# The last weight pieces of a decode kernel: full rows of 128 on all DMA engines in place of a piece for three engines alone

## The chip, the cores and the metric

One core of one Trainium2 chip. The time is the device time of a whole execution in microseconds (us), median of several runs; the span of the profile is some 1.3 us shorter.

## The reference, cut to what matters

A decode step for 4 tokens: gated mix of a windowed attention over a key and value cache and a gated feed-forward. What matters here is how much must be loaded and what comes last.

```python
q = (x @ wq)                                   # 32 heads of 128
o = softmax(q k^T * 128**-0.5) v               # last 4096 positions, 4 batches x 8 kv heads
a = o.reshape(4, 4096) @ wo                    # wo is 4096 x 512, bf16: 4 MB
b = ((relu(x @ W_gate)) * (x @ W_up)) @ W_down
out = g * a + (1 - g) * b
```

Some 81 MB are read: keys and values, five weight matrices. `wo` is used last and is loaded last.

## The kernel before

The load order ends with `W_down` and then `wo`, all issued from SyncE. `wo` lies in SBUF as 128 rows (partitions) of 32 KB, in 64 columns of 512 B, and comes in pieces of columns, so that the matmuls of one piece run while the next piece lands:

```python
WO_PIECES = ((0, 34), (34, 52), (52, 60), (60, 63), (63, 64))
LOW3 = (0, 123, 126, 128)
...
def wo_rows(p):
    return [slice(a, b) for a, b in zip(LOW3, LOW3[1:])] if p == len(WO_PIECES) - 1 else [slice(0, 128)]
...
for n, r in enumerate(wo_rows(it[1])):
    load(("WO", it[1], n), f"d_wo{it[1]}", Wo[r, OW * lo:OW * hi], wo[r, OW * lo:OW * hi], waits=w)
```

The last column is cut into 123, 3 and 2 rows, which puts it on the three lowest DMA engines alone; the other thirteen have 4 KB less to do. TensorE adds all columns into one accumulator, even columns into its first half and odd ones into its second. The two halves are placed on different parts of the array, so that two neighbouring columns run side by side (in the trace of before the second of a pair starts 3 to 4 ns after the first):

```python
def WO(p):
    lo, hi = WO_PIECES[p]
    w = [("WO", p, n) for n in range(len(wo_rows(p)))] + [("E", "OQ")]
    for x in range(lo, hi):
        i, j = x // OUTT, x % OUTT
        mm(banks[ACC][OR * j:OR * j + 4, 0:OW], oq[:, i, :], Wo[:, OW * x:OW * x + OW], False, i == 31,
           ev=("WOP", p) if x == hi - 1 else None, waits=w if x == lo else (), pos=(0, OR * j))
```

ScalarE copies the first half and VectorE the second, and then the output is stored. TensorE's order before the wo pieces is: last attention value product (PV), down projection of the feed-forward (FFN), fold of the heads (OQ). After OQ, VectorE scales the heads into `oq`, which all wo matmuls need.

Of the kernel before, what the change touches and what calls it, by code (L numbers as in the profile page):

```python
# [24 lines left out]
OUTT = 2  # L25
OW = 512 // OUTT
OR = 128 // OUTT
WO_PIECES = ((0, 34), (34, 52), (52, 60), (60, 63), (63, 64))
LOW3 = (0, 123, 126, 128)

class _Plan:

# [17 lines left out]
def bc(ap, axis, n):  # L50
    shape = list(ap.shape)
    shape[axis] = n
    return ap.broadcast_to(shape)
# [31 lines left out]
def bass_gated_mix__sliding_block_cached__glu_gated_reglu__decode_kernel(  # L85
    nc, A_x, A_k_cache, A_v_cache, A_wq, A_wo, B_x, B_W_gate, B_W_up, B_W_down, gate_w, out
):
    plan = _Plan()
    aps = (A_x, A_k_cache, A_v_cache, A_wq, A_wo, B_W_gate, B_W_up, B_W_down, gate_w, out)
    with ExitStack() as ctx:  # L90
        R = _alloc(nc, ctx)
        progs = _program(nc, plan, R, aps)
        for _, prog in progs:
            prog(None)
        for name in plan.unit:
            plan.sems[name] = ctx.enter_context(nc.semaphore(name))
        plan.emit, plan.n = True, {}
        if True:
            for name, prog in progs:
                prog(getattr(nc, name))  # L100
# [46 lines left out]
def _order():  # L147
# [7 lines left out]
    o += [("SC", s, 3), ("SW", s), ("PV", s - 1), ("PT", s), ("RS", 1), ("GU",), ("PV", s), ("FFN",), ("OQ",)]  # L155
    return o + [("WO", p) for p in range(len(WO_PIECES))]


def _dma_order():
    o = [("wq",), ("x",), ("gw",), ("k", 0), ("k", 1), ("v", 0)]  # L160
    for s in range(2, NSET):
        o += [("k", s), ("v", s - 1)]
    return o + [("wg",), ("wu",), ("v", NSET - 1), ("wd",)] + [("wo", p) for p in range(len(WO_PIECES))]

# [22 lines left out]
def _program(nc, plan, R, aps):  # L187
# [14 lines left out]
    def slot(*it):  # L202
        return slots[:, at[it], :]
# [4 lines left out]
    Wo = slot("wo", 0)  # L208
# [19 lines left out]
    def tr(key):  # L228
        return TR[trf[key] % NTR]
# [5 lines left out]
    def scb(key):  # L235
        return SCB[scf[key] % NSC]
# [2 lines left out]
        n = scf[key] - NSC  # L239
        return [("E",) + sck[n]] if n >= 0 else [("INIT",)]  # L240

    def wo_rows(p):

        return [slice(a, b) for a, b in zip(LOW3, LOW3[1:])] if p == len(WO_PIECES) - 1 else [slice(0, 128)]

    def set_of(s):
        return s % 4, s // 4

    def ob(s):
        return banks[OB[s % 2]]  # L250

    def sync(e):
        E = _Eng(plan, e, "sp")

        def load(ev, ctr, dst, src, waits=()):
            E.op(lambda: e.dma_start(dst, src), ev=ev, waits=waits, ctr=ctr)  # L256

        for it in _dma_order():
            k = it[0]
            w = slot_wait.get(it, [])  # L260
            if k == "x":
                load(("X",), "d_x", xsb[0:4, :], A_x.rearrange("b o d -> (b o) d"))
            elif k == "gw":
                load(("GW",), "d_gw", xsb[4:5, :], gate_w.rearrange("(o p) -> o p", o=1))
            elif k == "wq":
                load(("WQ",), "d_wq", slot("wq"), A_wq.rearrange("(p t) f -> p (t f)", t=4), waits=w)
            elif k == "wg":
                load(("WG",), "d_wg", Wg, B_W_gate.rearrange("(p t) f -> p (t f)", t=4), waits=w)
            elif k == "wu":
                load(("WU",), "d_wu", Wu, B_W_up.rearrange("(p t) f -> p (t f)", t=4), waits=w)  # L270
            elif k == "wd":
                load(("WD",), "d_wd", Wd, B_W_down.rearrange("(p i) c -> p (i c)", i=14),
                     waits=w)
            elif k == "wo":
                lo, hi = WO_PIECES[it[1]]
                wo = A_wo.rearrange("(p i) c -> p (i c)", i=32)
                for n, r in enumerate(wo_rows(it[1])):
                    load(("WO", it[1], n), f"d_wo{it[1]}", Wo[r, OW * lo:OW * hi], wo[r, OW * lo:OW * hi], waits=w)
            else:
                b, qq = set_of(it[1])  # L280
                src = (A_k_cache if k == "k" else A_v_cache)[b, 4 * qq:4 * qq + 4, SK - WIN:SK, :]
                load((k.upper(), it[1]), f"d_{k}{it[1] % 3}", slot(*it), src.rearrange("h (r c) d -> r h (c d)", r=32),
                     waits=w)
        load(("OUT",), "d_out", out.rearrange("b o d -> (b o) d"), osum[:, :], waits=[("OSUM", 1), ("OSUM", 0)])
        E.wait([("OUT",)])
# [30 lines left out]
    def tensor(t):  # L316
        E = _Eng(plan, t, "pe")

        def mm(out_, lhsT, rhs, start, stop, ev=None, waits=(), pos=None):
            E.op(lambda: t.matmul(out_, lhsT, rhs, start=start, stop=stop, tile_position=pos, skip_group_check=True),  # L320
                 ev=ev, waits=waits)
# [101 lines left out]

        def WO(p):
            lo, hi = WO_PIECES[p]
            w = [("WO", p, n) for n in range(len(wo_rows(p)))] + [("E", "OQ")]
            for x in range(lo, hi):
                i, j = x // OUTT, x % OUTT
                mm(banks[ACC][OR * j:OR * j + 4, 0:OW], oq[:, i, :], Wo[:, OW * x:OW * x + OW], False, i == 31,
                   ev=("WOP", p) if x == hi - 1 else None, waits=w if x == lo else (), pos=(0, OR * j))  # L430

        fns = dict(CONST=CONST, XT=XT, Z=Z, Q=Q, QT=QT, SC=SC, PV=PV, SW=SW, RS=RS, OQ=OQ, WO=WO, GU=GU, FFN=FFN)
        for it in order:
            if it[0] in fns:
# [41 lines left out]
    def q_dst(n, u):  # L476
        return (pe, sc)[n][:, :].rearrange("p (x u w) -> p x u w", x=8, u=4)[:, :, u, :]

    def q_src(n):
        return banks[scb(("Q", n))].rearrange("p (x w) -> p x w", x=8)  # L480

    def vector(v):
# [93 lines left out]
        def FIN():  # L576
            E.op(lambda: v.tensor_copy(osum[:, OW:2 * OW], banks[ACC][OR:OR + 4, 0:OW]), ev=("OSUM", 1),  # L577
                 waits=[("WOP", len(WO_PIECES) - 1)])

# [5 lines left out]
    def scalar(a):  # L585
        E = _Eng(plan, a, "act")

        def EQ(n):
            key = ("Q", n)
            E.op(lambda: a.activation(q_dst(n, slice(0, 4)), bc(q_src(n).unsqueeze(2), 2, 4), ACTF.Copy), ev=("QD", n),  # L590
                 waits=[key])
            plan.ev[("E", "Q", n)] = plan.ev[("QD", n)]

        def ECONST(k):
            key = ("CONST", k)
            dst = consts[k]
            E.op(lambda: a.activation(dst[:, :], banks[tr(key)][:, 0:dst.shape[1]], ACTF.Copy), ev=("E",) + key, waits=[key])

        def GWB():
            E.op(lambda: a.activation(R["gwB"][:, :, :], bc(xT[:, 4:20:5].unsqueeze(2), 2, 128), ACTF.Copy), ev=("GWB",),  # L600
                 waits=[("E", "XT")])

        def NORM(s):
            E.op(lambda: a.activation(osb[:, s, :], ob(s), ACTF.Copy), ev=("NORM", s),  # L604
                 waits=[("PV", s)])

        def GE():
            for u in range(2):
                E.op(lambda u=u: a.activation(ge[:, u, :], banks[ACC][:, 0:4], ACTF.Exp, scale=-1.0 if u == 0 else 1.0),
                     ev=("GE",) if u else None, waits=[("Z",)])  # L610

        def RELU():
            E.op(lambda: a.activation(grelu, banks[scb(("GU", 0))][:, 0:448], ACTF.Relu), ev=("RELU",),
                 waits=[("GU", 0), ("EXP", NSET - 1)])
            plan.ev[("E", "GU", 0)] = plan.ev[("RELU",)]

        def EXP(s):
            w = [("NEGMAX", s), ("E", "SC", s, 3)] + ([("E", "PT", s - 1)] if s else [("QT", 1, 1)])
            E.op(lambda: a.activation(pe[:, :], sc[:, :], ACTF.Exp, bias=negmax[:, s % 2:s % 2 + 1], scale=SCALE,  # L619
                                      accum_out=rowsum[:, s:s + 1]), ev=("EXP", s), waits=w)  # L620

        def FIN():
            E.op(lambda: a.activation(osum[:, 0:OW], banks[ACC][0:4, 0:OW], ACTF.Copy), ev=("OSUM", 0),
                 waits=[("WOP", len(WO_PIECES) - 2)])

        fns = dict(ECONST=ECONST, GWB=GWB, EQ=EQ, GE=GE, RELU=RELU, EXP=EXP, NORM=NORM, FIN=FIN)
        for it in act:
            fns[it[0]](*it[1:])

    return [("tensor", tensor), ("vector", vector), ("scalar", scalar), ("gpsimd", gpsimd), ("sync", sync)]  # L630


# [26 lines left out]
```

## Time and profile before

| | before |
|---|---|
| time | 196.12 us (196.02 to 196.21) |
| span of the profile | 194.8 us |
| read from memory | 81.01 MB at 416 GB/s over the span |
| the one load queue | 97.3% of its 16 engines' span |
| TensorE, VectorE, ScalarE busy | 62%, 64%, 14% |

Some words used from here on: a load is split over DMA engines; each sends a 4 B semaphore packet after its own data, and that shows as one *count* on the load's semaphore. The last count is the *landing*. A *late* engine is one whose counts come some 0.8 us or more behind those of the others.

These are lines of the timeline of before: start us, duration us, engine, line of the program (here the helper that issues every matmul), operation and operands, count, and in brackets how long the engine sat idle and what ended it.

```profile
178.49 5.03 PE L320 MATMUL bank<-slots,pT 128*64 128x512 bf16 x32 [5.70 <-DMA slots<-in_A_v_cache_dram]
183.45 1.69 PE L320 MATMUL bank<-slots,hg 128*4 128x256 bf16 x28
185.07 1.93 PE L320 MATMUL bank<-osb,fold 128*64 128x256 bf16 x16
...
188.07 2.02 PE L320 MATMUL bank<-slots,oq 128*4 128x256 bf16 x34 [1.06 <-DMA slots<-in_A_wo_dram]
190.83 1.15 PE L320 MATMUL bank<-slots,oq 128*4 128x256 bf16 x18 [0.73 <-DMA slots<-in_A_wo_dram]
192.20 0.82 PE L320 MATMUL bank<-slots,oq 128*4 128x256 bf16 x12 [0.23 <-DMA slots<-in_A_wo_dram]
```

PV, FFN, OQ, then the wo pieces.

### The profile page before, as it was taken

Reading aid. Unit: us, or ns where it says so; the run is one execution under the profiler, and the core shown is the slowest. Engines: PE = TensorE matmul, PEld = TensorE weight load, DVE = VectorE, ACT = ScalarE, POOL = GpSimd, SP = SyncE. Lnnn points to the kernel's source line nnn. Section 1 sums busy time; section 2 is a strip of 40 time slices with the busy share of each in tenths; the row PEclk is TensorE's granted clock in tenths of the full one; section 3 lists DMA queues with packets and bytes.
Section 4 is the critical chain, followed back from the end, with each engine's and each line's share of the span. In section 5 each row is a group of like instructions: output and inputs, shape, how many; then the busy total and the mean of one; then the engine's idle time right before and its main releaser. Section 6 shows DMA issues by size and latency. Waiting matters only on the chain.

```text
span 194.8 us, 1734 instructions
## 1 busy us (share of the span) xinstructions
PE 120.6 (62%) x723; PEld 50.6 (26%) x723; DVE 124.1 (64%) x153; ACT 27.5 (14%) x34; POOL 9.5 (5%) x25
## 2 busy tenths in 40 slices
PE   0209279474943894686468943894586466743974
PEld 0003123121411341242112411341142122311562
DVE  6103769999399809980998199819981998370010
ACT  2213000040130013001300130013001300420100
POOL 7830000000000000000000000000000000000000
PEclk9999958999999797899876999697999889997899
DMA  6999999999999999999999999999999999999992
GB/s 215 431 432 431 437 437 431 431 427 451 431 437 437 446 427 424 431 437 431 431 431 431 427 424 437 444 437 431 431 431 421 431 395 427 470 431 384 425 404 90
DMA packets 3616, 81.10 MB, mean 416 GB/s; under 512 B 401, under 2 KB 666, under 8 KB 794
## 3 DMA queue, kind: packets, MB, share of 16 engines
q1 hardware_dynamic: 3610, 81.01, 97.3%
q8 instruction: 5, 0.08, 0.2%
q14 instruction: 1, 0.01, 0.0%
HBM read 81.01 MB, written 0.00 MB: 416 GB/s over the span
## 4 chain that ended last, share of the span: by engine, by line
DMA 54%; DVE 31%; PE 9%; issue 4%; SPq 0%; ACT 0%
DMA slots<-in_A_k_cache_dram 38%; DVE kt L491 21%; DMA slots<-in_A_wo_dram 10%; PE bank L320 7%; DMA xsb<-in_A_x_dram 6%; DVE sc L527 5%; DVE qblk L517 1%; PE bank L324 1%; DVE pT L542 1%; DVE rd L531 1%; SPq L256 0%; DVE negmax L537 0%; ACT gwB L600 0%; DVE osum L577 0%; DVE mx L527 0%
## 5 line engine op out<-in xcount | busy, mean ns | idle before, releaser
L491 DVE STREAM_TRANSPOSE kt<-slots 128x2048 f32<-128x2048 f32 x32 | 73.7, 2305 | 28.1 <-DMA slots<-in_A_k_cache_dram 28.0
L320 PE MATMUL bank<-kt,qblk 128*128 128x512 bf16 x256 | 72.1, 434 | 27.9 <-DVE kt L491 27.9
L320 PEld LDWEIGHTS bank<-kt,qblk 128*128 128x128 bf16 x256 | 25.2, 107 | 69.7 <-DVE kt L491 36.0
L320 PE MATMUL bank<-slots,pT 128*64 128x512 bf16 x256 | 32.3, 410 | 5.7 <-DMA slots<-in_A_v_cache_dram 5.7
L619 ACT ACTIVATE pe<-sc,negmax 128x2048 bf16<-128x2048 bf16 x8 | 16.0, 2002 | 60.1 <-DVE negmax L537 60.1
L527 DVE CUSTOM_DVE_ANT_0 sc<-bank,maskf 128x512 bf16<-128x512 f32 x32 | 21.0, 658 | 3.8 <-PE bank L320 3.7
L320 PEld LDWEIGHTS bank<-slots,pT 128*64 128x64 bf16 x256 | 15.1, 118 | 23.2 <-issue 13.4
L542 DVE STREAM_TRANSPOSE pT<-pe 128x2048 bf16<-128x2048 bf16 x8 | 18.5, 2312 | 2.2 <-ACT pe L619 2.2
L604 ACT ACTIVATE osb<-bank 128x512 bf16<-128x512 f32 x8 | 4.8, 597 | 81.5 <-PE bank L320 81.5
L320 PE MATMUL bank<-rd,grpb 128*128 128x32 bf16 x8 | 1.6, 194 | 22.1 <-DVE rd L531 22.1
L555 DVE TENSOR_TENSOR oq<-bank,recip 64x128 bf16<-64x128 f32 x2 | 0.9, 434 | 12.3 <-PE bank L320 12.2
L320 PEld LDWEIGHTS bank<-rd,grpb 128*128 128x128 bf16 x8 | 0.8, 98 | 25.7 <-DVE rd L531 25.7
L495 DVE COPY xT<-bank 128x20 bf16<-128x20 bf16 x1 | 0.2, 171 | 8.0 <-PE bank L324 8.0
L320 PE MATMUL bank<-slots,oq 128*4 128x256 bf16 x64 | 4.0, 272 | 2.0 <-DMA slots<-in_A_wo_dram 2.0
L320 PE MATMUL bank<-slots,xT 128*4 128x512 bf16 (+1 forms) x64 | 5.0, 467 | 0.0
L320 PE MATMUL bank<-maskr,maskl 128*128 128x512 bf16 x1 | 0.6, 609 | 5.9 <-POOL maskr L296 5.9
L517 DVE TENSOR_SCALAR qblk<-bank 32x64 uint32<-32x64 uint32 x16 | 2.9, 215 | 2.1 <-PE bank L324 2.1
L324 PE MATMUL bank<-identb,xsb 5*128 5x5 bf16 x4 | 0.3, 168 | 5.7 <-DMA xsb<-in_A_x_dram 5.7
L577 DVE CAST osum<-bank 4x256 bf16<-4x256 f32 x1 | 0.4, 418 | 5.2 <-PE bank L320 5.2
L320 PEld LDWEIGHTS bank<-slots,oq 128*4 128x4 bf16 x64 | 2.5, 84 | 3.5 <-DMA slots<-in_A_wo_dram 2.9
L296 POOL TENSOR_SCALAR_AFFINE_SELECT fold<-fold 128x256 bf16<-128x256 bf16 x8 | 3.3, 417 | 1.1
L486 DVE MEMSET qblk<- 128x2304 uint32 x1 | 2.0, 1978 | 1.3 <-PEq L644 1.3
(59 smaller groups left out, 40.3 us busy)
## 6 DMA issues: line engine op xcount, KB each, us to landing
slots<-in_A_k_cache_dram SPq DMA_DIRECT2D x8, 4096.0 KB, 25.1
slots<-in_A_v_cache_dram SPq DMA_DIRECT2D x8, 4096.0 KB, 30.5
slots<-in_A_wq_dram SPq DMA_DIRECT2D x1, 4096.0 KB, 12.4
slots<-in_A_wo_dram SPq DMA_DIRECT2D x1, 2176.0 KB, 17.1
slots<-in_B_W_gate_dram SPq DMA_DIRECT2D x1, 1792.0 KB, 19.7
slots<-in_B_W_up_dram SPq DMA_DIRECT2D x1, 1792.0 KB, 23.6
slots<-in_B_W_down_dram SPq DMA_DIRECT2D x1, 1792.0 KB, 18.5
slots<-in_A_wo_dram SPq DMA_DIRECT2D x1, 1152.0 KB, 19.5
```

The source lines that it names most:

```text
L296: op(lambda: e.affine_select(dst, src, pattern, cmp, fill, base=base, channel_multiplier=mult), ev)
L320: E.op(lambda: t.matmul(out_, lhsT, rhs, start=start, stop=stop, tile_position=pos, skip_group_check=True), ev=ev, waits=waits)
L324: E.op(lambda: t.transpose(out_, in_, idn), ev=ev, waits=waits)
L486: E.op(lambda: v.memset(qblk[:, :, :, :, :].rearrange("p s h c e -> p (s h c e)"), 0.0), ev=("QZ",))
L491: E.op(lambda: v.transpose(kt[:, f, :].bitcast(FP32), slot("k", s)[:, 4096 * f:4096 * f + 4096].bitcast(FP32)), ev=("E", "KT", s, f), waits=w)
L517: E.op(lambda dst=dst, r=r, g=g: v.tensor_scalar(dst, src[r, g, 0:B, :, :], 0, None, op0=ALU.bitwise_or), ev=("E",) + keys[1] if (q, g) == ...
L527: E.op(lambda: v.tensor_tensor_reduce(sc[:, 512 * f:512 * f + 512], banks[scb(key)], R["maskf"][:, :], 1.0, -3.0e38, ALU.add, ALU.max, mx4 ...
L531: E.op(lambda: v.tensor_tensor(rd32[:, :, :], bc(R["own8"][:, :].unsqueeze(2), 2, 4), bc(mx4[:, :].unsqueeze(1), 1, 8), ALU.mult), ev=("MA ...
L542: E.op(lambda: v.transpose(pT[:, s % 2, :], pe[:, :]), ev=("E", "PT", s), waits=[("EXP", s)] + ([("PV", s - 2)] if s >= 2 else []))
L555: E.op(lambda g=g, r=r: v.tensor_tensor(oq[r, :, :].rearrange("p i b -> p b i"), banks[tr(key)][0:64, 128 * g:128 * g + 128].rearrange("p ...
L604: E.op(lambda: a.activation(osb[:, s, :], ob(s), ACTF.Copy), ev=("NORM", s), waits=[("PV", s)])
L619: E.op(lambda: a.activation(pe[:, :], sc[:, :], ACTF.Exp, bias=negmax[:, s % 2:s % 2 + 1], scale=SCALE, accum_out=rowsum[:, s:s + 1]), ev= ...
```

## The change

The intent is to drop the special piece: five pieces in full rows of 128, so that all 16 engines end together, with a last piece of 1 KB rows.

```diff
-WO_PIECES = ((0, 34), (34, 52), (52, 60), (60, 63), (63, 64))
-LOW3 = (0, 123, 126, 128)
+WO_PIECES = ((0, 35), (35, 52), (52, 59), (59, 62), (62, 64))
@@
-                for n, r in enumerate(wo_rows(it[1])):
-                    load(("WO", it[1], n), f"d_wo{it[1]}", Wo[r, OW * lo:OW * hi], wo[r, OW * lo:OW * hi], waits=w)
+                load(("WO", it[1]), f"d_wo{it[1]}", Wo[:, OW * lo:OW * hi], wo[:, OW * lo:OW * hi], waits=w)
@@
-            w = [("WO", p, n) for n in range(len(wo_rows(p)))] + [("E", "OQ")]
+            w = [("WO", p), ("E", "OQ")]
@@ (ScalarE's closing copy)
-                 waits=[("WOP", len(WO_PIECES) - 2)])
+                 waits=[("WOP", len(WO_PIECES) - 1)])
```

More of the change, by code (lines that the diff above doesn't have):

```diff
@@ L240, in sc_free @@
         return [("E",) + sck[n]] if n >= 0 else [("INIT",)]
-    def wo_rows(p):
-        return [slice(a, b) for a, b in zip(LOW3, LOW3[1:])] if p == len(WO_PIECES) - 1 else [slice(0, 128)]
     def set_of(s):
```

## The prediction

> **What bounds the kernel now.** I read the page's busy rows first, then the chain of work that ended last, then the stretches of the last microseconds, then the DMA issues, and last the trace's own records of single packets and of completion counts.
>
> ```profile
> DMA  6999999999999999999999999999999999999992
> q1 hardware_dynamic: 3610, 81.01, 97.3%
> DMA 54%; DVE 31%; PE 9%; issue 4%; SPq 0%; ACT 0%
> ```
>
> The DMA row is at 9 in 38 of 40 slices, and the one queue fills 97.3% of its 16 engines' span. The 81 MB set the time; DVE and PE in the chain are work that lets the next load start, not a bound of their own. The change moves no byte away, so only how the bytes end, engine by engine, can matter. The end of the chain of work says what ends last:
>
> ```profile
> 171.74 20.41 DMA slots<-in_A_wo_dram
> 192.16 0.04 issue
> 192.20 0.87 PE bank L320 x12
> 193.07 0.02 issue
> 193.09 0.42 DVE osum L577
> ```
>
> From the third-last wo piece (landed 192.16) on, only twelve matmuls, one copy and the store are left. The stretches of those microseconds (columns: us, busy of PE, PEld, DVE, ACT, POOL, granted clock, DMA share, GB/s) show the engines dropping out one after another, not together:
>
> ```profile
> 189.00:190.00 1.00, 1.00 (x21) 0.67 (x16) 0.00 (x0) 0.00 (x0) 0.00 (x0) 1.00 0.99 399
> 190.00:191.00 1.00, 0.27 (x6) 0.15 (x6) 0.00 (x0) 0.00 (x0) 0.00 (x0) 1.00 0.73 273
> 191.00:192.00 1.00, 0.97 (x18) 0.56 (x14) 0.00 (x0) 0.00 (x0) 0.00 (x0) 1.00 0.39 132
> ```
>
> So the end belongs to a few late engines. The completion counts in the trace give the rest. The 1.5 KB-row piece (the fourth) is counted by ten engines from 190.70 to 191.23, by one at 191.88, and by five from 192.35 to **192.60**. The eight counts of the last, 512 B-row piece come from 191.87 to **192.39**. Thus the last landing is the fourth piece's on the late engines, not the last piece's on the low three: the low three have some 0.2 us to spare.
>
> Why five or six are late is also in the trace. Beside 81 MB of data there are five 16 KB instruction packets (1.02 to 1.07 us each, at 40.2, 73.0, 111.7, 148.2 and 182.1 us) and one of 8 KB at 63.3. After each, one more of the 16 counts of the next big load is late: by some 1.4 us after a 16 KB packet in the middle of the run, and by 0.9 us after the 8 KB one. They stay late to the end.
>
> **What the Trainium skill says.**
> 1. "DMA: Bandwidth & Descriptors", section "Why a DMA increments its semaphore by 16 and not by 1": a DMA issued here runs on the largest number of engines up to 16 that divides its outer dimension, the lowest-numbered ones; 128 rows give 16. So 123 rows should run on 3, 3 rows on 3, and 2 rows on 2. The trace agrees: 8 landings for the last piece, plus three jumps at its issues. The 512 B packets run as three interleaved streams starting at 190.30, 190.31 and 190.32.
> 2. Same page, section "Why small descriptors are slow (HBM only)": a fixed cost per packet. The trace agrees, and its sizes are used below: the step from packet to packet on one engine is 23.5 ns at 512 B, 61.2 at 1536 B, 155.4 at 4096 B, about 646 at 17408 B. A line through these is 4.6 ns + 0.0369 ns per byte, so an estimate for 1 KB is 42.3 ns.
> 3. Same page, section "Anatomy of one DMA — SWDGE (gpsimd) path": most of a DMA's fixed cost of about 2 us is the receipt of the last write. This kernel's loads are not of that path; the trace has 0.48 us from the late engine's last semaphore packet (ends 192.118) to its count (192.596). I use 0.48.
>
> **The change part by part.** Wo has 64 column pieces of 512 B in each row; every engine serves 8 rows.
>
> *Removed:* the 123, 3 and 2 row transfers of 512 B rows: 43 or so packets of 23.5 ns on each of the three low engines, about 1.0 us there. They lie beside the late engines' work and end 0.2 us before them, so on the path they are worth 0. Also two issues by SyncE; its last two groups are issued at 173.05 (10.32 us long) and 183.42 (1.31), so all is issued by 184.8, while the first 512 B packet starts at 190.30. Worth 0.
>
> *Added:* 512 B more per row on all the other 13 engines, in 5 pieces of full rows instead of 4. Per row, on a late engine:
> - before 17408 + 9216 + 4096 + 1536 B: 4 x 4.6 + 0.0369 x 32256 = 1208.6 ns
> - after 17920 + 8704 + 3584 + 1536 + 1024 B: 5 x 4.6 + 0.0369 x 32768 = 1232.1 ns
>
> The difference is 23.5 ns; 8 rows make 188 ns, and one more 4 B semaphore packet (about 9 ns) makes **0.197 us**. The last landing goes from 192.60 to about 192.79.
>
> *Moved:* what PE does after it. Before, the fourth piece's three matmuls and the last piece's one start 0.041 us after 192.596, in two pairs (192.637 and 192.747), and the last is over at 193.023: 0.427 us from landing to end. After, the last piece has two matmuls, which start as one pair (one writes each half of the accumulator): 0.041 + 0.004 + 0.272 = 0.317 us. So 0.110 us come back. Is PE free by then? The third piece now ends at 236 KB of 256 KB per engine instead of 240, the fourth at 248 instead of 252: both about 0.15 us sooner, 192.01 and 192.45. Seven matmuls in four pairs of 0.109 us from 192.05 are through at 192.49, three more at about 192.71, before 192.83. PE is free, and the landing alone counts.
>
> *The closing copies:* ACT now waits for the last piece, as DVE always did. ACT's copy began at 193.056 and DVE's at 193.090, with 0.373 and 0.418 us (the two osum rows); DVE ends last now and will after. Worth 0. The store after it is the same.
>
> Sum: +0.197 - 0.110 = **+0.087 us**. On a median of 196.12 that is 196.2, 0.04% slower, which is inside the spread of the three runs of before (196.02 to 196.21).
>
> The instruction listing of the two kernels shows the same number of rows on PE, DVE, ACT and POOL and two fewer on SP; PE's 723 matmuls stay. Nothing before the wo loads changes.
>
> **The rivals.**
> - *The low three engines did set the end, and freeing them is a gain.* Then the time would fall by up to the 0.2 us by which I have them early, to about 195.9. Against: the 12 matmuls run with the last one paired to its neighbour (it starts 4 ns after it), so it waited for nothing of its own. A weaker form of it: three streams of 512 B reads disturb the late engines. Between 191.06 and 191.42 packets of all sizes take longer (4096 B up to 199 ns instead of 159), some 0.1 us in all on a late engine. If the small packets cause this, the change gives 0.1 back and ends at 196.1. Against: the three streams run 0.7 us before that without any such effect.
> - *The small packets cost more than the line says.* 13 engines now end in eight 1 KB packets. The only 1 KB packets of the trace, in the store, are 46 to 52 ns long. At 52 instead of 42, eight rows add 0.08 us: 196.3.
> - *The instruction packets fall elsewhere.* If one engine got two of them, it would be another 1.3 us late, and the time 197.5. If they held no engine up at the end, the last landing could come some 1.4 us sooner, with the ten early ones: 194.8. For this: nothing says how an engine is chosen. Against: PE's instruction stream, which needs most of the fetching, keeps its count, and six packets met six different engines. I give it one chance in twenty.
>
> **How the range and the chances follow.** The worked sum gives 196.21; the weaker rival pulls it to 196.1 and the second pushes it to 196.3; runs of one kernel lie within 0.1 of their median. Another day's run of the same kernel may differ by another 0.2 or so (a guess). So 195.9 to 196.5 in 8 of 10 cases. Being 2% off would take 3.9 us; no term above is larger than the 1.4 of an instruction packet. So within 2%: 0.98; faster and slower 0.01 each.
>
> **What would show it right or wrong.** In the issues of the profile after: the 192 KB piece lands near 192.45, and a 128 KB piece near 192.79 (both within 0.1 us), with 16 counts, five or six late ones among them. In the stretch from 191 to 192 the DMA share rises a little. In the chain, PE's last group has two or five matmuls, and the copy by DVE starts near 193.18. I am wrong in mechanism if the last landing comes at or before 192.60, if PE waits longer than 0.05 us after it, or if ACT's copy ends after DVE's; and wrong in size if a 1 KB step is not near 42 ns, or if the late engines are not the same number.

## The result, and the profile after

| | before | after |
|---|---|---|
| time, median | 196.12 us (196.02 to 196.21, 6 runs) | 196.11 us (195.94 to 196.19, 6 runs) |
| ratio of the fast runs | | 0.9998, 95% interval 0.9985 to 1.0011 |
| span of the profile | 194.8 us | 194.7 us |

A ratio is the mean time of one kernel's fast runs over that of the other's in the same rounds, so it is not quite the ratio of the medians; all ratios in this document are against the kernel before. The change made no difference that the timing could resolve (0.13%, or 0.25 us).

The load queue of after looks as it did, in the page's busy row and its queue row:

```profile
DMA  6999999999999999999999999999999999999992
q1 hardware_dynamic: 3618, 81.01, 97.3%
```

The end of the chain of work does not (start us, duration us, what):

```profile
188.63 0.45 DVE oq L549
189.08 0.14 issue
189.21 3.69 PE bank L314 x64
192.90 0.02 issue
192.92 0.42 DVE osum L571
```

Where before had a DMA of 20.41 us and then twelve matmuls, this trace has all 64 wo matmuls in one run of 3.69 us behind VectorE's scaling; no load is in the last part of the chain. The timeline of after shows why: its first lines answer to those of before.

```profile
178.51 6.15 PE L314 MATMUL bank<-slots,pT 128*64 128x512 bf16 x32 [5.73 <-DMA slots<-in_A_v_cache_dram]
184.59 1.69 PE L314 MATMUL bank<-slots,hg 128*4 128x256 bf16 x28
186.21 1.94 PE L314 MATMUL bank<-osb,fold 128*64 128x256 bf16 x16
...
189.21 3.67 PE L314 MATMUL bank<-slots,oq 128*4 128x256 bf16 x64 [1.06 <-DVE oq L549]
```

PV started at the same time but took 6.15 us instead of 5.03, so everything behind it came 1.1 us later, and the wo pieces were there when TensorE came. In the stretches (us, busy of PE, PEld, DVE, ACT, POOL with counts, granted clock, DMA share, GB/s) the clock of before and then of after is

```profile
178.40:183.00 4.60, 4.51 (x30) 2.45 (x32) 0.00 (x0) 0.00 (x0) 0.00 (x0) 0.68 1.01 425
```

```profile
178.40:183.00 4.60, 4.49 (x22) 2.32 (x24) 0.00 (x0) 0.00 (x0) 0.00 (x0) 0.50 1.01 425
```

0.68 against 0.50 of full clock in the same stretch. It is not the change that made that: in the repeats below the kernel before has 0.50 too, and the kernel after 0.66.

The loads end one after another as before, in the stretches of after:

```profile
189.00:190.00 1.00, 0.79 (x16) 0.68 (x18) 0.07 (x1) 0.00 (x0) 0.00 (x0) 1.00 0.97 386
190.00:191.00 1.00, 1.00 (x24) 0.83 (x20) 0.00 (x0) 0.00 (x0) 0.00 (x0) 1.00 0.73 273
191.00:192.00 1.00, 1.00 (x24) 0.83 (x20) 0.00 (x0) 0.00 (x0) 0.00 (x0) 1.00 0.35 128
```

The DMA share falls as before (there 0.99, 0.73 and 0.39), while TensorE has no gap. The completion counts show 10 early and 6 late engines again. The last landing is at 192.563 us, 0.033 **earlier** than in before (192.596) where 192.79 was foretold. So two things had to be found out: what took the 0.2 us away, and how often TensorE, not the loads, sets the end.

### The profile page after: what moved, and what is told of

It reads as the page before. It is cut to its first block, busy times and chain, and to the rows that moved or that the text cites. A ratio compares the mean times of both kernels' runs of the same rounds, so it can differ in the third digit from the quotient of the medians.

```text
span 194.7 us, 1732 instructions
## 1 busy us (share of the span) xinstructions
PE 122.7 (63%) x723; PEld 51.9 (27%) x723; DVE 124.6 (64%) x153; ACT 27.5 (14%) x34; POOL 9.5 (5%) x25
## 4 chain that ended last, share of the span: by engine, by line
DMA 46%; DVE 25%; PE 21%; issue 6%; SPq 0%; ACT 0%
DMA slots<-in_A_k_cache_dram 25%; PE bank L314 19%; DVE kt L485 18%; DMA slots<-in_A_v_cache_dram 15%; DMA xsb<-in_gate_w_dram 6%; DVE sc L521 4%; PE bank L318 2%; DVE qblk L511 1%; DVE oq L549 0%; DVE rd L525 0%; DVE negmax L531 0%; SPq L251 0%; ACT gwB L594 0%; DVE osum L571 0%; DVE mx L521 0%
## 5 line engine op out<-in xcount | busy, mean ns | idle before, releaser
L314 PE MATMUL bank<-slots,pT 128*64 128x512 bf16 x256 | 34.0, 426 | 5.7 <-DMA slots<-in_A_v_cache_dram 5.7
L314 PEld LDWEIGHTS bank<-slots,pT 128*64 128x64 bf16 x256 | 15.7, 123 | 24.9 <-issue 15.8
```

The costliest lines, as they stand in the source:

```text
L314: E.op(lambda: t.matmul(out_, lhsT, rhs, start=start, stop=stop, tile_position=pos, skip_group_check=True), ev=ev, waits=waits)
```

## The experiments

All outputs were correct. Besides the times, each run gives one trace, from which these are read: the last landing, the start of the wo matmuls, and single packets.

### Both kernels once more: chance or change?

No edit: `rep_before`, `rep_after` (3 rounds each), and later one single look each, `rep2_before` and `rep2_after`.

> The kernel before once more, unchanged, for a second trace. Theory A (the worked +0.197 us on a given late engine is right, and in the two traces it was cancelled by chance: which engine the last instruction packet hit, and a 0.1 us slowing at 191.06 to 191.42): the last landing of the 1.5 KB-row piece differs from 192.60 by more than 0.05 us, and packets of 180 ns and more near 191 us need not come back. Rival B (the change itself takes the 0.2 us away, for example because the 512 B streams on three engines slow the others): the last landing is 192.60 again within 0.05, with slow packets near 191.2 again. Time 196.1 under both.

> The kernel after once more, unchanged. Theory A: a late engine takes 5.35 us from the w_down landing to the first wo piece, as in the first trace of after (5.20 in that of before), but the last landing may lie anywhere from 192.5 to 192.9. Rival B: last landing 192.56 within 0.05. Where the granted clock in the stretch 178.4 to 183.0 is 0.5 again, PE runs 64 wo matmuls without a gap (3.7 us); where it is 0.7 or more, PE waits for the pieces. Time 196.1 under both.

> The kernel before, a third trace: slow packets near 191.3 again if the transfers on three engines make them; the last landing anywhere from 192.5 to 192.9 if chance moves it by 0.2 us.

> The kernel after, a third trace: no 3584 B packet over 160 ns after 190.0; the last landing anywhere from 192.5 to 192.9; PE without a gap in the wo stage where the clock of the stretch 178.4 to 183.0 is near 0.5.

Measured: 196.09 us (ratio 1.0001) and 196.13 us (0.9998, 0.9984 to 1.0013). The traces, with those of two later variants that have TensorE early (`before_ffn`; `ffn_split` and `ffn_split2`, further down):

| trace | clock 178.4 to 183.0 | wo matmuls start | waits among them | last landing | from it to the last matmul's end | first piece to last landing | longest 1536 B packet after 190.0 |
|---|---|---|---|---|---|---|---|
| before | 0.68 | 188.07 | yes | 192.596 | 0.427 us | 4.590 us | 95 ns |
| rep_before | 0.50 | 189.80 | none | 192.807 | 0.649 | 4.597 | 94 |
| rep2_before | 0.65 | 188.19 | yes | 192.704 | 0.428 | 4.618 | 87 |
| before_ffn | 0.69 | 188.05 | yes | 192.604 | 0.428 | 4.602 | 78 |
| after | 0.50 | 189.21 | none | 192.563 | 0.319 | 4.546 | 69 |
| rep_after | 0.66 | 188.29 | yes | 192.768 | 0.318 | 4.538 | 69 |
| rep2_after | 0.50 | 189.53 | none | 192.814 | 0.374 | 4.552 | 67 |
| ffn_split | 0.53 | 188.22 | yes | 192.721 | 0.321 | 4.545 | 67 |
| ffn_split2 | 0.50 | 188.54 | yes | 192.642 | 0.319 | 4.540 | 67 |

"First piece to last landing" runs from the last count of the first wo piece to the last landing of all. The rest is in microseconds from the span's start.

Three readings. First, the last landing moves by 0.2 us among traces of one kernel (192.60 to 192.81 and 192.56 to 192.81), so the early landing of the first trace of after was within chance. Rival B, that the landing is fixed for each kernel, is out.

Secondly, a part is not chance: first piece to last landing is 4.59 to 4.62 us in all of the old scheme and 4.54 to 4.55 in all of the new, though a late engine moves the same 14848 B per row in it under both (9216 + 4096 + 1536, and 8704 + 3584 + 1536 + 1024). With one packet per row and one semaphore packet more, the new scheme should take 0.046 us longer there, and it takes some 0.06 less. The slow packets come back in every trace of the old scheme and in none of the new.

They are not the whole of it. The packets can be linked to engines by their times. On the engine that lands last, the time from the end of the first piece's semaphore packet to the end of the last one is 4.575 us on average under both schemes (4.56 to 4.60 and 4.57 to 4.58). There the slow packets cost 0.03 to 0.07 us in the old scheme, and at most 0.02 in the new, which about pays for the extra packet per row. The other 0.06 us lie between semaphore packets and counts: on average 0.44 us after the first piece and 0.47 after the last in the old scheme, 0.46 and 0.43 in the new. No run shows what sets that delay.

Thirdly, where the clock was 0.5 in the two kernels as they are, TensorE ran its 64 wo matmuls without a wait, and where it was 0.65 or more it waited. In rep_before this cost time:

```profile
189.66 0.14 issue
189.80 3.70 PE bank L320 x64
193.50 0.02 issue
193.52 0.42 DVE osum L577
```

Its landing was over at 192.81, but its last matmul ended 0.65 us later, and this was the slowest of its four executions (196.51 us; the others 196.03 to 196.14). In rep_after the loads set the end, as the prediction had it:

```profile
171.46 19.43 DMA slots<-in_A_wo_dram
190.89 0.04 issue
190.94 2.17 PE bank L314 x29
193.10 0.02 issue
193.13 0.42 DVE osum L571
```

### full512: the sizes of before, all in full rows

```diff
-WO_PIECES = ((0, 35), (35, 52), (52, 59), (59, 62), (62, 64))
+WO_PIECES = ((0, 34), (34, 52), (52, 60), (60, 63), (63, 64))
```

(against after)

> After with the piece sizes of before: 17, 9, 4, 1.5 and 0.5 KB rows, all five on 128 rows; so it is before with the last piece spread over all 16 engines. Theory B' (transfers on few engines slow the packets of the others near 191 us; small packets as such don't): no packet of 4096 B over 172 ns and none of 1536 B over 72 ns after 190.0. Rival: the 512 B packets themselves do it, then slow ones come back in as many numbers as in the two traces of before. Last landing 0.18 after the 1.5 KB piece, anywhere from 192.6 to 192.9. Time 196.1 (within 0.15) under both.

Measured: 196.16 us, ratio 1.0001 (0.9987 to 1.0014). In its trace the clock was 0.50 again, and TensorE, not the loads, set the end (64 wo matmuls in one run from 189.43, the last over 0.66 us after the landing), so the packets are what this run is read for. After 190.0 us no 4096 B packet is over 169 ns and no 1536 B packet over 68 ns, with 128 packets of 512 B on all engines. So 512 B packets do not slow the others; transfers that run on three engines do. The last landing was earlier than foretold (192.42), as chance and the lighter first piece have it. Its first piece to last landing is 4.692 us; the packet terms give 8 x (344.2 + 155.5 + 61.2 + 23.5) ns = 4.675 us, plus four semaphore packets of 9 ns: 4.71. For after they give 8 x (325.3 + 136.7 + 61.2 + 42.3) = 4.524, with four semaphore packets 4.56, and 4.54 to 4.55 were measured. For before they give 8 x (344.2 + 155.5 + 61.2) = 4.487, with three semaphore packets 4.51, and 4.59 to 4.62 were measured. The terms hold within some 0.02 us wherever all rows are full, and are **0.08 to 0.10 us** short where three engines get a piece of their own. Of that, 0.03 to 0.07 us are slow packets on the engine that lands last (0.01 in full512); the rest is the delay of the counts.

### low3_2k: four columns for the low three

```diff
-WO_PIECES = ((0, 34), (34, 52), (52, 60), (60, 63), (63, 64))
+WO_PIECES = ((0, 34), (34, 50), (50, 57), (57, 60), (60, 64))
```

(against before; ScalarE's copy waits for the last piece, as in after)

> The scheme of before with four columns (2 KB rows) left to the lowest three engines instead of one, all others ending at 240 KB. Theory A (the end follows the engine that lands last, at 4.6 ns + 0.0369 ns per byte for each packet): 43 packets of 80 ns are 3.45 us after 190.25, so the last landing is 193.73, the last matmul ends at 194.16 instead of 193.02, and the time rises by 1.1 us to 197.2. Rival C (the 16 engines share one rate, so that only total bytes count): no change, 196.1.

Measured: 197.71 us, ratio 1.0077 (1.0060 to 1.0094), so 1.6 us slower where 1.1 was foretold. Rival C, that only the total counts, is out: the bytes are the same. The end of the chain:

```profile
183.34 10.95 DMA slots<-in_A_wo_dram
194.29 0.04 issue
194.33 0.40 PE bank L320 x4
```

The end follows the engine that lands last, and the tail behind it is 0.43 us with its two pairs of matmuls. The landing came 0.56 us later than the packet terms said. Linked by their times, the 2048 B packets form three chains, of 43, 43 and 42. The chain that ended last took 3.69 us for its 43, where the terms give 3.44, so 0.25 us are slow packets: mostly 84 ns long, they went up to 155 ns between 190.4 and 191.6, and 1536 B and 3584 B ones of the other engines up to 135 and 211 ns in the same time. The slowing goes both ways. Another 0.14 us lie between the last semaphore packet and its count: 0.62 us here, against 0.48 in before for the fourth piece. The remaining 0.17 us were not traced; that chain's first packet began at 189.97.

### diag_k: which engines are late

```diff
+KS = (15, 14, 13, 12, 11, 10, 9, 8, 7, 6, 5, 4, 3, 2, 9)
+    def wo_rows(p):      # last piece: one transfer of KS[n] rows after the other, each with a semaphore
+        if p < len(WO_PIECES) - 1:
+            return [slice(0, 128)]
+        return [slice(sum(KS[:n]), sum(KS[:n + 1])) for n in range(len(KS))]
```

(against after)

> After, with the last piece (1 KB rows) cut into 15 transfers of 15, 14, 13 ... 2 and 9 rows, so that the n-row transfer has n landings on the n lowest engines. The number of late landings (over 0.8 us behind) in each tells which engines the instruction packets hit. If the low three are never hit, the 3-row and 2-row transfers have no late landing, and the number of late ones rises to 5 or 6 by 15 rows. If the hit engines are spread by chance, late ones appear in the small transfers too. The time is 196.1 to 196.6, as the lowest engine gets 15 KB.

Measured (one look): 198.29 us, some 2 us more than foretold. The data were not late: the last 1 KB packet ended at 192.17 us and the last semaphore packet at 192.18. The counts were.

```profile
177.75 16.65 DMA slots<-in_A_wo_dram
194.39 0.46 issue
```

The last counts of the transfers with 15, 14, 13 and 12 rows came at 192.62, 192.81, 193.00 and 193.19, and so on to 194.39, so counts of one engine followed each other at some 0.19 us even where its data were long there. Then TensorE took 0.46 us for its waits on fifteen semaphores. The low engines have up to three counts to give for the last piece of before and of low3_2k; that these follow each other in the same way would fit the long delay there (some 0.8 and 0.62 us), and was not tested apart.

What the run was for is the number of late counts among the n lowest engines:

| n | 15 | 14 | 13 | 12 | 11 | 10 | 9 | 8 | 7 | 6 | 5 | 4 | 3 | 2 |
|---|---|---|---|---|---|---|---|---|---|---|---|---|---|---|
| late | 6 | 6 | 6 | 6 | 5 | 4 | 3 | 3 | 3 | 2 | 1 | 1 | 0 | 0 |

Engines are numbered from 0 here, and an n-row transfer is taken to run on the n lowest, as the prediction has it. Then each step down tells one engine: 11, 10, 9, 6, 5 and 3 are late in this run. The low three are not, which is what the piece for them alone made use of. Six late engines and six instruction packets were found in every trace of before and of after, except that the sixth of rep_after was only some 0.75 us behind.

### oq_twice and ffn_split: is TensorE the second bound?

```diff
+            for again in range(2):        # oq_twice: the 16 matmuls of the head fold twice, same result
```

```diff
-... ("PV", s), ("FFN",), ("OQ",)]
+... ("PV", s), ("FFN", 0, 5), ("OQ",), ("FFN", 5, 14)]     # ffn_split
```

(each edit against after)

> After with the 16 matmuls of the head fold issued twice (same result), 1.94 us more PE work ahead of the wo stage and no other change. Theory D (PE's chain ends together with the landings): wo matmuls start at 190.1 or later and run without a gap for 3.7 us, so the end is 0.7 to 2.0 us later: 196.8 to 198.1. Rival (landings alone decide; PE has 2 us of waits to give in the trace of before): 196.1 to 196.3.

> After with the 28 down-projection matmuls split: 10 before the head fold (to cover ACT's copy of the last attention output) and 18 after it (to cover DVE's two scalings). The wo matmuls start about 0.9 us sooner. Theory D (PE's chain is a second bound of the tail that decides when the granted clock in 178 to 183 is near 0.5): PE now waits for the last piece in every trace, the end is last landing + 0.34, and the median falls by 0.1 to 0.3 us, to 195.8 to 196.0. Rival (landings alone decide): 196.1.

oq_twice took 197.55 us, ratio 1.0080 (1.0067 to 1.0092). Its head fold, and the end of its chain:

```profile
186.10 3.68 PE L314 MATMUL bank<-osb,fold 128*64 128x256 bf16 x32
...
190.71 0.14 issue
190.85 3.67 PE bank L314 x64
194.52 0.02 issue
```

The fold takes 3.68 us instead of 1.94, so the work added is 1.74 us, not the 1.94 of the expectation. It cost 1.5 us by the medians and 1.6 by the ratio. So TensorE had only some 0.2 us to give in the typical run, and rival "landings alone decide" is out.

ffn_split took 196.02 us, ratio 0.9994 (0.9981 to 1.0006). The trace does what it was made for: at a clock of 0.53 the wo matmuls start at 188.22 and wait for the pieces,

```profile
184.24 0.71 PE L314 MATMUL bank<-slots,hg 128*4 128x256 bf16 x10
184.99 1.93 PE L314 MATMUL bank<-osb,fold 128*64 128x256 bf16 x16
186.86 1.15 PE L314 MATMUL bank<-slots,hg 128*4 128x256 bf16 x18
188.22 2.13 PE L314 MATMUL bank<-slots,oq 128*4 128x256 bf16 x35 [0.21 <-DMA slots<-in_A_wo_dram]
```

and the end is 0.32 us after the last landing. The gain of 0.1 us in the ratio is not clear of the noise, so the expected gain of 0.1 to 0.3 us is neither shown nor excluded.

### before_ffn and ffn_split2: the change with TensorE out of the way

The edit of ffn_split on before, and ffn_split once more, on the same chip.

> Before with the split of ffn_split, so that PE is early and only landings can set the end. Theory A: last landing of the 1.5 KB piece at 192.6 to 192.8 with slow packets (over 172 ns at 4096 B) near 191.3, last matmul 0.43 us after it, end of the last copy 193.5 to 193.7; time 196.0 to 196.2, not to be told from ffn_split2 (within 0.15 us). Rival (the change is worth 0.2 us or more one way once PE is out of the way): the two differ by more than 0.2 us.

> The kernel ffn_split once more beside before_ffn on the same chip: after with PE early. Theory A: last landing 192.5 to 192.8, no slow packets, last matmul 0.33 us after it. Time 196.0, within 0.15 us of before_ffn.

Measured: 196.00 us, ratio 0.9990 (0.9977 to 1.0002), and 196.08 us, ratio 0.9995 (0.9982 to 1.0009); the kernel before had 196.28 in these rounds. In both traces the loads set the end (0.428 and 0.319 us after the landing). The two differ by 0.08 us, inside their spread. So even where only landings can set the end, the change is worth nothing that can be measured.

### low3_first: an attempt to beat both

```diff
-WO_PIECES = ((0, 35), (35, 52), (52, 59), (59, 62), (62, 64))
+WO_PIECES = ((0, 35), (35, 53), (53, 59), (59, 61), (61, 62), (62, 64))   # (61, 62): low three, loaded last, used before (62, 64)
```

(against ffn_split, with the 123, 3 and 2 rows of before for the one column)

> An attempt to beat both: the split of ffn_split, and the low-three piece of before again, but on a column whose matmul comes ahead of the last pair, so that after the late engines' last landing (252 KB each) only one pair of matmuls is left. By the terms: against ffn_split -0.15 for 4 KB less per late engine, +0.1 for the slowing by the few-engine streams, so within 0.1 of it; against before -0.11 for the pair. 195.8 to 196.1; rival: 196.1 as all else.

Measured: 196.00 us, ratio 0.9994 (0.9982 to 1.0007), last landing 192.585. It is not told from the others. None of the variants beats both kernels clearly.

## Why the prediction was right or wrong

The time (196.11 against 196.2 foretold) and "no change" were right. Step by step:

- **Bound by loads, end set by late engines:** right, as low3_2k shows: one engine group later by some 1.7 us in landing moves the time by 1.5 to 1.6.
- **+0.197 us for the late engines:** right in its packet terms, too large in its sum. The step from the `W_down` landing to the first wo piece (mean of the first eight counts) is 5.19 to 5.20 us in the four traces of the old scheme and 5.34 to 5.38 in the five of the new, near the +0.151 us of the larger first piece. Packets of 1 KB are mostly 46 ns long; with the 4 ns by which the durations of the other sizes exceed their steps this is the 42 ns used. But from there on the new scheme does not lose 0.046 us, it gains 0.06.
- **The term that was mis-sized** is this one, by 0.105 us. A part is what the first rival's weaker form named and the prediction then argued away: the streams on three engines slow the others. Its argument, that the three streams ran 0.7 us before without effect, was wrong as evidence. The slowing is there in every trace with such a piece and absent in every one without; full512 shows that it is not the small packets. Its size, which the prediction read as "some 0.1 us", is 0.047 us on the last engine of before and 0.03 to 0.07 over the four traces, some 0.04 more than under the new scheme. The other 0.06 us is the delay from semaphore packet to count, which the prediction took as 0.48 us throughout; it was 0.41 to 0.50 after the first and last pieces, and why it differs stays open. Taken in, the late engines lose 0.197 - 0.105 = 0.09 us.
- **-0.110 us for the last pair of matmuls:** right. From landing to the end of the last matmul it is 0.427 to 0.428 us in before wherever loads set the end, and 0.318 to 0.321 in after. VectorE's copy starts 0.067 us after it in before (193.023 to 193.090) and 0.042 in after (192.882 to 192.924), a further 0.025 that was not foretold (0.067 to 0.069 and 0.040 to 0.042 in all traces of the two schemes). So the repaired sum is +0.092 - 0.110 - 0.025 = **-0.04 us**. The times can't tell this from the +0.087 foretold: their interval, -0.29 to +0.22 us, holds both, and with TensorE out of the way the new scheme was 0.08 us slower, inside the spread. What is shown is that the terms of 0.1 us cancel too nearly for any run here to see.
- **"PE is free, and the landing alone counts":** wrong for part of the executions. It rested on one trace with a granted clock of 0.68. In three of the six traces of the two kernels the clock was 0.50, TensorE reached the wo stage 1.1 to 1.7 us later than in before and ran it without a wait. In the first trace of after both chains tie (0.319 us after the landing, as if loads had set the end); in rep2_after TensorE adds 0.05 us and in rep_before 0.22. It hits both kernels alike, so it does not show in the comparison, but it can add to their spread (not tested apart).
- **"Wrong in mechanism if the last landing comes at or before 192.60":** it did, at 192.563, and this test was badly chosen. The landing varies by 0.2 us from trace to trace of one kernel; the means are 192.68 for the four traces of the old scheme and 192.70 for the five of the new, and a difference of 0.09 cannot be seen in so few. Where the variation comes from was not settled; that the last instruction packet meets an engine that is more or less behind already would fit, and was not tested. The other signs went the same way: in the first trace of after the 192 KB piece landed at 192.24 (192.45 foretold), VectorE's copy began at 192.92 (193.18) and the DMA share from 191 to 192 fell to 0.35 instead of rising; in rep_after the landings were 192.49 and 192.77 and the copy began at 193.13, near what was foretold.
- **Instruction packets elsewhere:** did not come to pass; no trace showed one engine with two of them.

What makes streams on few engines slow the others stays open: no run separated the memory side from the SBUF side.

## What to carry to other kernels

When loads bound a kernel, its end belongs to the engine that lands last plus whatever is left to compute after that landing; count both for each engine, since here 512 B more per row on the late engines and one pair of matmuls in the tail were each worth some 0.1 us, and cancelled. A piece given to a few early engines was not free here, as it slowed packets of the others while it ran. Many small transfers on one engine were not free either: their counts came one after another, 0.19 us apart. And before calling a second engine free, look at more than one trace: its clock may differ from run to run.

## What the Trainium skill lacked or had wrong

- "DMA: Bandwidth & Descriptors", section "Issuing engines are not separate DMA queues", says that all transfers share the same 16 engines; no page gives a size for how much a load confined to few engines slows the packets of the others. Here 4096 B packets went from 159 to as much as 199 ns and 1536 B ones from 65 to 95, which cost the last engine 0.03 to 0.07 us; with 2 KB rows on three engines, 3584 B packets went from 140 to as much as 211 ns.
- "Runtime: NRT & Kernel Launch", section "Instruction fetch mechanics", says that instructions are fetched in 16 KiB blocks and that the cost of crossing from one to the next is mostly hidden. The size agrees (five packets of 16384 B, and one of 8192 B). In this kernel, bound by loads, the cost is not hidden: after each such packet (1.02 to 1.11 us) one DMA engine more is late, by some 1.3 to 1.5 us, and stays so to the end; six of 16 engines ended late.
- No page says which engines fetch instructions. In diag_k the late ones were 3, 5, 6, 9, 10 and 11.
- "DMA: Bandwidth & Descriptors", section "Anatomy of one DMA — SWDGE (gpsimd) path", puts the fixed cost near 2 us, mostly the receipt of the last write. For these loads from SyncE the landing came 0.41 to 0.48 us after the last semaphore packet in full rows, some 0.8 us for the piece on three engines in before, and 0.62 in low3_2k. No page gives the time between the counts of successive transfers on one engine; in diag_k it was some 0.19 us.
- No page says that one issue can take as long as here: the 123-row transfer kept SyncE for 10.3 us in before, where each full-row wo piece of after took 0.33 to 0.44 us and the transfers of 2 to 15 rows in diag_k 0.25 to 0.38. Why was not tested. It cost nothing here.
